# Output stores of a one-core attention and MLP kernel: from GpSimd's queue to SyncE's, with one add and one transfer for each quarter of a batch

## The chip, the cores and the metric

The kernel runs on one core of one Trainium2 chip. The metric is the device time of one execution in microseconds (us). The engines are called as in the profile: PE is TensorE's matmuls, PEld its weight loads, DVE is VectorE, ACT ScalarE, POOL GpSimd, SP SyncE. "Granted clock" is the share of its full clock that TensorE got.

The kernel before was run many times. At first its times were 780.05 us as the median of 3 runs, 780.04 to 781.94. All runs in this document are called fast: none was 1.5% above the fastest of its kernel. Within "fast", however, the kernel before has two levels, near 780.2 and near 781.8, and this will matter.

## The reference, cut to what matters

```python
B, H, S, Ns, D = (8, 8, 512, 32, 64)          # x: [B,H,S,D], state: [B,H,Ns,D], FP32
a     = softmax(scale * x @ state.T);  xread = a @ state        # per batch and head
a2    = softmax(scale * state @ x.T);  sread = a2 @ x
t     = concatenate([xread, sread], axis=2)                      # -> [B*(S+Ns), H*D] = [4352, 512]
h     = t @ w_in                                                 # 512 -> 2048
g     = h * sigmoid(1.702 * h)
out   = g @ w_out                                                # 2048 -> 512, FP32
```

Each batch gives 512 rows of 512 for x and 32 rows for the state. All eight batches' state rows are treated together, under the key "sr".

Of the kernel before, what the change touches and what calls it, by code (L numbers as in the profile page):

```python
# [14 lines left out]
ALU = mybir.AluOpType  # L15
# [5 lines left out]
def kernel(  # L21
# [31 lines left out]
    nc = tc.nc  # L53

    B, H, S, D = x.shape
    Ns = state.shape[2]
# [11 lines left out]
    HF, HN = NF // 2, DM // 2  # L68
# [4 lines left out]
    out_x = out.rearrange("(b t) n -> b t n", b=B)[:, :S].rearrange("b (c q) n -> b c q n", c=SCH)  # L73
    out_s = out.rearrange("(b t) n -> b t n", b=B)[:, S:]
# [43 lines left out]
    def load_state(b):  # L118
        stn[b] = apool.tile([P, NG, D], FP32, tag="stn", name=f"stn_{b}", bufs=2)
        for g in range(NG):  # L120
            nc.sync.dma_start(stn[b][:, g], st_v[b, g])  # L121

    def load_x(b):
        if b == 1:
            xn[b] = sums[:, 0].rearrange("p (c h d) -> p c h d", c=SCH, h=H)
        else:
            xn[b] = xpool.tile([P, SCH, H, D], FP32, tag="xn", name=f"xn_{b}")
        for c in range(SCH):
            nc.sync.dma_start(xn[b][:, c], x_v[b, c])  # L129
# [252 lines left out]
    def att_slots(b):  # L382

        slots = [[] for _ in range(14)]

        def at(i, fn, *args):
            slots[i].append((fn, args))

        at(0, att_state, b)
        for j in range(NPR):  # L390
            at(j, att_xT, b, j)

        at(5, att_scores, b)
        at(5, att_M, b, 0)
        at(5, att_M, b, 1, True)
        at(5, att_blocks, b)
        at(5, att_s_max, b)
        at(5, att_s_exp, b)
        at(5, att_x_exp, b)
        at(5, att_s_norm, b)  # L400
        at(5, att_x_norm, b)
        at(8, att_M, b, 2)
        at(8, att_M, b, 3, True)
        for g in range(NG):
            at(10 + g, att_eT, b, g)
        at(12, att_sread, b)
        at(13, att_srT, b)
        return slots
# [13 lines left out]
    def up_x(b, f, spare=False):  # L422
        c, o = divmod(P * f, FC)
        m = A[b]["M", c]
        up(b, f, S, [m[:, g, o : o + P] for g in range(NG)], [A[b]["aT"][:, g] for g in range(NG)], spare)

    def up_s(f):
        up(
            "sr", f, B * Ns,
            [w_in_of(k, f) for k in range(NPR)],  # L430
            [srT[:, k].rearrange("p b n -> p (b n)") for k in range(NPR)],
        )
# [3 lines left out]
    def down(key, r, fs, dst, last):  # L436

        if fs[0] == 0:
            O[key, r] = psO.tile([P, DM], FP32, tag="o", name=f"o_{key}_{r}")
        ops = O[key, r]  # L440
        for f in fs:
            nc.tensor.matmul(  # L442
                ops, G[key, f][:, P * r : P * (r + 1)], w_out[:, f], start=(f == 0), stop=(f == NF - 1)
            )
            if last and f < HF:
                free.append(G.pop((key, f)))
        if fs[-1] == NF - 1:
            osb = opool.tile([P, DM], FP32, tag="osb", name=f"osb_{key}_{r}")
            nc.scalar.copy(osb, ops)
            nc.gpsimd.dma_start(dst, osb)  # L450


    S1, S2 = (later[:, 4 * i : 4 * i + 4].rearrange("p f n -> p (f n)").rearrange("p (f t) -> p f t", f=HF) for i in range(2))
# [2 lines left out]
    def quarters(key, f, ntok):  # L456

        g, half = G[key, f], ntok // 2
        return g[:, :half], g[:, half:ntok]

    def sums_of_g(key, f, ntok):

        half = ntok // 2
        (a11, a21), (_, a22) = quarters(key, f, ntok), quarters(key, HF + f, ntok)
        s1, s2 = S1[:, f, :half], S2[:, f, :half]
        nc.vector.tensor_tensor(out=s1, in0=a21, in1=a22, op=ALU.add)  # L466
        nc.vector.tensor_tensor(out=a21, in0=a11, in1=a21, op=ALU.subtract)
        nc.vector.tensor_tensor(out=s2, in0=s1, in1=a11, op=ALU.subtract)

    def strassen(key, ntok, dst, slots=None):  # L470
        half = ntok // 2
        nb = half // P
        B11, B21, B22 = w_out[:, :HF, :HN], w_out[:, HF:, :HN], w_out[:, HF:, HN:]
        T3 = w_out[:, :HF, HN:]
        A = lambda i, k: [quarters(key, HF * k + f, ntok)[i] for f in range(HF)]
        S = lambda t: [t[:, f, :half] for f in range(HF)]
        todo = list(slots or [])

        def bank(name):
            return psO.tile([P, nb, HN], FP32, tag="o", name=f"{name}_{key}")  # L480

        def product(ps, lhs, rhs, first):
            for r in range(nb):
                for f in range(HF):
                    nc.tensor.matmul(  # L485
                        ps[:, r], lhs[f][:, P * r : P * (r + 1)], rhs[:, f],
                        start=(first and r == 0 and f == 0), stop=(f == HF - 1), skip_group_check=True,
                    )
                if todo:
                    for fn, args in todo.pop(0):  # L490
                        fn(*args)

        def kept(t):
            return t[:, : nb * HN].rearrange("p (r n) -> p r n", r=nb)

        def store(i, k, ps, with_):

            o = opool.tile([P, nb, HN], FP32, tag="osb", name=f"osb_{key}_{i}{k}")
            for r in range(nb):
                if with_ is None:  # L500
                    nc.scalar.copy(o[:, r], ps[:, r])  # L501
                else:
                    nc.vector.tensor_tensor(out=o[:, r], in0=ps[:, r], in1=with_[:, r], op=ALU.add)  # L503
                nc.gpsimd.dma_start(dst(nb * i + r, slice(HN * k, HN * (k + 1))), o[:, r])  # L504

        k1, k2, k3 = kept(p1), kept(u2), kept(u3)
        X = bank("x")
        product(X, A(0, 0), B11, True)
        nc.scalar.copy(k1, X)
        Y = bank("y")  # L510
        product(Y, S(S2), T2, True)
        nc.vector.tensor_tensor(out=k2, in0=Y, in1=k1, op=ALU.add)  # L512
        product(X, A(0, 1), B21, False)
        store(0, 0, X, None)
        for f in range(HF):
            a12 = quarters(key, HF + f, ntok)[0]
            nc.vector.tensor_tensor(out=a12, in0=a12, in1=S2[:, f, :half], op=ALU.subtract)
        product(Y, A(1, 0), T3, False)
        nc.vector.tensor_tensor(out=k3, in0=Y, in1=k1, op=ALU.add)
        for f in range(HF):  # L520
            free.append(G[key, f])
        Z = bank("z")
        product(Z, S(S1), T1, True)
        store(1, 1, Z, k3)
        product(Y, A(1, 1), T4, False)
        store(1, 0, Y, k1)
        product(Z, A(0, 1), B22, False)
        store(0, 1, Z, k2)
        for f in range(HF, NF):
            free.append(G[key, f])  # L530
# [86 lines left out]
    for f in range(NF):  # L617
        rounds(1)
        round_to(NFC * NPR + f + 1)
        for r in range(SCH):  # L620
            down(0, r, [f], out_x[0, r], r == SCH - 1)
        if f in (0, 2):
            for g in range(NG):
                att_eT(f // 2, g)
        if f in (0, nper * 2):
            att_M(1, 2 + f // (nper * 2))
        if f in (1, 3):
            att_sread(f // 2)
        if f in (2, 4):
            att_srT(f // 2 - 1)  # L630
        if f % 2 == 1:
            up_x(1, rest.pop(0))
        if f == NF - 2:
            T_of(T1, B12, B11)
            for k in range(HF - 1):
                sums_of_g(1, k, S)
            T_of(T2, B22, T1)
# [6 lines left out]
    nb = P // Ns  # L644
    for b in range(1, B):
        ahead = b + 1 < B
        if not ahead:
            for f in range(NF):
                up_s(f)
                if f >= HF:  # L650
                    sums_of_g("sr", f - HF, B * Ns)
            strassen("sr", B * Ns, lambda r, n: out_s[nb * r : nb * (r + 1), :, n])
        if b > 1:
            for f in range(NF):
                up_x(b, f)
                if f >= HF:
                    sums_of_g(b, f - HF, S)
        strassen(b, S, lambda r, n: out_x[b, r][:, n], att_slots(b + 1) if ahead else None)
        if b + 2 < B:
            load_state(b + 2)  # L660
            load_x(b + 2)
# [30 lines left out]
```

## The kernel before: the parts that the change touches

A batch's loads are issued from SyncE's queue. The x of a batch takes four transfers of 256 KB, the state two of 32 KB:

```python
def load_state(b):
    stn[b] = apool.tile([P, NG, D], FP32, tag="stn", name=f"stn_{b}", bufs=2)
    for g in range(NG):
        nc.sync.dma_start(stn[b][:, g], st_v[b, g])
def load_x(b):
    ...                                       # xpool has one buffer; b == 1 lies elsewhere
    for c in range(SCH):
        nc.sync.dma_start(xn[b][:, c], x_v[b, c])
```

Batch 0's second layer is computed directly (`down`); each of its four row blocks is copied out of PSUM by ScalarE and stored by GpSimd. All other batches use Strassen's scheme, which yields the output in quarters (128 partitions, 2 row blocks, 256 columns). Each quarter is stored as two halves:

```python
# in down():
        osb = opool.tile([P, DM], FP32, tag="osb", name=f"osb_{key}_{r}")   # opool: 2 buffers
        nc.scalar.copy(osb, ops)
        nc.gpsimd.dma_start(dst, osb)
# in strassen():
    def store(i, k, ps, with_):
        o = opool.tile([P, nb, HN], FP32, tag="osb", name=f"osb_{key}_{i}{k}")
        for r in range(nb):
            if with_ is None:
                nc.scalar.copy(o[:, r], ps[:, r])
            else:
                nc.vector.tensor_tensor(out=o[:, r], in0=ps[:, r], in1=with_[:, r], op=ALU.add)
            nc.gpsimd.dma_start(dst(nb * i + r, slice(HN * k, HN * (k + 1))), o[:, r])
```

The order in which the program emits the parts around batch 2's first use is this:

```python
for f in range(NF):                            # second layer of batch 0, NF = 16
    rounds(1); round_to(NFC * NPR + f + 1)     # last weights: loaded on SyncE, rounded
    for r in range(SCH):
        down(0, r, [f], out_x[0, r], r == SCH - 1)   # f == 15 stores
    ...
load_state(2)                                  # emitted AFTER batch 0's four stores
load_x(2)
for b in range(1, B):
    ...
    strassen(b, S, ..., att_slots(b + 1))      # the slots hold the next batch's attention:
    if b + 2 < B:                              # slot 0 transposes its state and x on PE
        load_state(b + 2)
        load_x(b + 2)
```

## Time and profile before

| what | kernel before, profiled run |
|---|---|
| device time of the profiled run; span of its trace | 782.2 us; 780.4 us |
| PE busy; mean granted clock | 763.8 us (98%); 0.995 |
| DVE, ACT, POOL busy | 314.4, 219.1, 35.9 us |
| PE's last matmul ends; span ends | 772.50; 780.41 (7.91 us later) |
| stores: POOL | 60 (56 of 128 KB, 4 of 256 KB), and 4 of the state rows |
| loads of batch 2: issued; used | 123 to 128; 165.6 |

The span begins with the first instruction and ends with the last; the device time is 1.7 to 2.1 us longer in all runs here. The stretch from PE's last matmul to the end of the span is called the tail below: 7.91 us here. The profile's lines for the stores, the tail, SP's queue and the stretch near 160 us are shown in the prediction.

One view was not opened before the prediction, and should have been. It is the table of windows: the busy time of each engine, then the granted clock (the third number from the right), the DMA share and GB/s.

```profile
42.00:43.00 1.00, 0.40 (x1) 0.32 (x2) 0.93 (x3) 1.00 (x3) 0.00 (x0) 0.92 0.00 0
44.00:45.00 1.00, 1.00 (x2) 0.33 (x1) 0.96 (x3) 0.00 (x0) 0.00 (x0) 0.50 0.00 0
46.00:47.00 1.00, 1.00 (x4) 0.52 (x3) 1.00 (x4) 0.77 (x2) 0.00 (x0) 0.88 0.00 0
```

The clock is halved from 42.8 to 46.2, 3.4 us (a window at 0.92 has 0.16 us of half clock in it, one at 0.88 has 0.24), after a gap of 2.1 us on PE (40.5 to 42.6). So the profiled run belongs to the upper level, while the median from which the prediction set out, 780.05, belongs to the lower.

### The profile page before, as it was taken

What the parts mean: (1) busy time and instruction counts of PE and PEld (TensorE: products, weight loads), DVE (VectorE), ACT (ScalarE), POOL (GpSimd) and SP (SyncE); (2) the same over time, 40 slices, a digit from 0 to 9 for tenths busy, and PEclk for the clock granted to TensorE, in tenths of its full rate; (3) what the DMA queues carried; (4) which work ended last, traced back from release to release, by engine and by line L of the source; (5) the groups of instructions that cost most, each with busy time, mean ns of one, the idle gap of its engine ahead of it and who ended that gap; (6) DMA issues with size and microseconds to landing.
All of it is one profiled execution on the core that took longest, in us unless ns stands there. A gap on an engine that the chain in (4) does not pass through costs nothing.

```text
span 780.4 us, 9330 instructions
## 1 busy us (share of the span) xinstructions
PE 763.8 (98%) x3883; PEld 509.1 (65%) x3883; DVE 314.4 (40%) x669; ACT 219.1 (28%) x394; POOL 35.9 (5%) x72
## 2 busy tenths in 40 slices
PE   8989999999999999999999999999999999999995
PEld 3433444477855786487847785587748788874885
DVE  5998799534304160317113440407031611313120
ACT  4666511023132132314132313314232312113000
POOL 0000000010100011000100010001100010010011
PEclk9999999999999999999999999999999999999999
DMA  9821245010030003000210013000300000010001
GB/s 229 316 82 51 84 142 136 0 55 12 30 71 1 1 28 85 0 1 14 66 33 0 1 35 78 1 1 28 81 0 1 14 28 14 1 28 1 0 21 34
DMA packets 43626, 35.21 MB, mean 45 GB/s; under 512 B 37312, under 2 KB 37312, under 8 KB 43584
## 3 DMA queue, kind: packets, MB, share of 16 engines
q1 hardware_dynamic: 40000, 25.69, 12.1%
q0 software_dynamic: 3584, 8.92, 3.5%
q8 instruction: 30, 0.49, 0.3%
q14 instruction: 12, 0.10, 0.0%
HBM read 25.69 MB, written 8.91 MB: 44 GB/s over the span
## 4 chain that ended last, share of the span: by engine, by line
issue 69%; PE 22%; POOL 4%; SPq 2%; ACT 1%; DMA 1%; POOLq 0%; DVE 0%; ACTq 0%
PE h L417 8%; PE o L442 7%; POOL out_dram L504 4%; PE y L485 2%; PE x L485 2%; PE M L274 1%; SPq L129 1%; PE z L485 1%; PE warm L113 1%; DMA sums<-in_x_dram 1%; PE xT L256 0%; SPq L121 0%; PE s L274 0%; SPq L158 0%; ACT later L186 0%
## 5 line engine op out<-in xcount | busy, mean ns | idle before, releaser
L417 PE MATMUL h<-aT,M 128*128 128x512 f32 x512 | 225.7, 598 | 4.4 <-ACT M L349 4.4
L417 PEld LDWEIGHTS h<-aT,M 128*128 128x128 f32 x512 | 96.7, 191 | 127.3 <-issue 114.2
L419 ACT ACTIVATE g<-h 128x512 f32<-128x512 f32 x120 | 71.4, 596 | 161.9 <-PE h L417 161.8
L485 PE MATMUL x<-w_out,g 128*128 128x256 f32 x448 | 100.0, 379 | 0.0
L485 PEld LDWEIGHTS x<-w_out,g 128*128 128x128 f32 x448 | 84.2, 190 | 13.9 <-issue 3.3
L466 DVE TENSOR_TENSOR later<-g,g 128x256 f32<-128x256 f32 (+1 forms) x64 | 26.1, 408 | 149.7 <-ACT g L419 149.7
L349 ACT COPY M<-M 128x512 f32<-128x512 f32 x64 | 33.2, 596 | 94.9 <-PE M L274 94.9
L504 POOL DMA_DIRECT2D out_dram<-osb x56 | 30.0, 541 | 528.3 <-ACT osb L501 360.2
L485 PE MATMUL z<-w_out,g 128*128 128x256 f32 x224 | 51.1, 382 | 0.0
L485 PE MATMUL z<-sums,later 128*128 128x256 f32 x224 | 51.1, 382 | 0.0
L485 PE MATMUL y<-sums,later 128*128 128x256 f32 x224 | 50.5, 379 | 0.0
L485 PE MATMUL y<-sums,g 128*128 128x256 f32 x224 | 50.5, 379 | 0.0
L485 PE MATMUL y<-w_out,g 128*128 128x256 f32 x224 | 50.1, 382 | 0.0
L485 PEld LDWEIGHTS y<-w_out,g 128*128 128x128 f32 x224 | 42.1, 190 | 10.5 <-issue 5.0
L485 PEld LDWEIGHTS z<-sums,later 128*128 128x128 f32 x224 | 42.1, 190 | 10.5 <-issue 5.0
L485 PEld LDWEIGHTS y<-sums,g 128*128 128x128 f32 x224 | 42.1, 190 | 5.5
L485 PEld LDWEIGHTS z<-w_out,g 128*128 128x128 f32 x224 | 41.6, 190 | 5.7
L485 PEld LDWEIGHTS y<-sums,later 128*128 128x128 f32 x224 | 41.6, 190 | 5.2
L503 DVE TENSOR_TENSOR osb<-z,later 128x256 f32<-128x256 f32 x28 | 10.6, 419 | 78.6 <-PE z L485 78.6
L512 DVE TENSOR_TENSOR later<-y,later 128x512 f32<-128x512 f32 x7 | 4.8, 691 | 87.8 <-PE y L485 87.8
L274 PE MATMUL M<-w_in,stT 64*32 64x512 f32 x512 | 33.2, 594 | 0.2 <-ACT eT L359 0.2
L257 ACT COPY xT<-xT 128x512 f32<-128x512 f32 x28 | 16.4, 586 | 59.1 <-PE xT L256 59.1
(111 smaller groups left out, 707.1 us busy)
## 6 DMA issues: line engine op xcount, KB each, us to landing
later<-in_moe_w_out_dram SPq DMA_DIRECT2D x16, 512.0 KB
xn<-in_x_dram SPq DMA_DIRECT2D x28, 256.0 KB
out_dram<-osb POOLq DMA_DIRECT2D x56, 128.0 KB, 2.0
w_out<-in_moe_w_in_dram SPq DMA_DIRECT2D x12, 512.0 KB
later<-in_moe_w_in_dram SPq DMA_DIRECT2D x4, 512.0 KB
sums<-in_x_dram SPq DMA_DIRECT2D x4, 256.0 KB
out_dram<-osb POOLq DMA_DIRECT2D x4, 256.0 KB, 2.4
stn<-in_state_dram SPq DMA_DIRECT2D x16, 32.0 KB
```

The lines of the kernel that those rows point to most:

```text
L113: nc.tensor.matmul(ps, zeros[:, :P], zeros, start=True, stop=True)
L129: nc.sync.dma_start(xn[b][:, c], x_v[b, c])
L257: nc.scalar.copy(A[b]["xT"][:, j], ps.rearrange("p c q -> p (c q)"))
L274: nc.tensor.matmul(ps[g][st], A[b]["stT"][rows, st], rhs(rows, j), start=True, stop=True)
L349: nc.scalar.copy(m[:, g], ps[g])
L417: nc.tensor.matmul(hps, lhs[i], rhs[i], start=(i == 0), stop=(i == n - 1))
L419: nc.scalar.activation(out=gt[:, :ntok], in_=hps, func=AF.Gelu_apprx_sigmoid)
L442: nc.tensor.matmul(ops, G[key, f][:, P * r : P * (r + 1)], w_out[:, f], start=(f == 0), stop=(f == NF - 1))
L466: nc.vector.tensor_tensor(out=s1, in0=a21, in1=a22, op=ALU.add)
L485: nc.tensor.matmul(ps[:, r], lhs[f][:, P * r : P * (r + 1)], rhs[:, f], start=(first and r == 0 and f == 0), stop=(f == HF - 1), skip_grou ...
L503: nc.vector.tensor_tensor(out=o[:, r], in0=ps[:, r], in1=with_[:, r], op=ALU.add)
L504: nc.gpsimd.dma_start(dst(nb * i + r, slice(HN * k, HN * (k + 1))), o[:, r])
```

## The change

The intent is to take the stores off GpSimd's queue, which the page lists as `software_dynamic` (8.92 MB before), and to halve the number of adds and transfers. The adding lines and the place of the loads stay as they are.

```diff
@@ down
             nc.scalar.copy(osb, ops)
-            nc.gpsimd.dma_start(dst, osb)
+            nc.sync.dma_start(dst, osb)
@@ strassen, store
-            for r in range(nb):
-                if with_ is None:
-                    nc.scalar.copy(o[:, r], ps[:, r])
-                else:
-                    nc.vector.tensor_tensor(out=o[:, r], in0=ps[:, r], in1=with_[:, r], op=ALU.add)
-                nc.gpsimd.dma_start(dst(nb * i + r, slice(HN * k, HN * (k + 1))), o[:, r])
+            if with_ is None:
+                nc.scalar.copy(o, ps)
+            else:
+                nc.vector.tensor_tensor(out=o, in0=ps, in1=with_, op=ALU.add)
+            nc.sync.dma_start(dst(slice(nb * i, nb * (i + 1)), slice(HN * k, HN * (k + 1))), o)
@@ the two callers: dst takes a slice of row blocks instead of a number
```

More of the change, by code (lines that the diff above doesn't have):

```diff
@@ L651 @@
                     sums_of_g("sr", f - HF, B * Ns)
-            strassen("sr", B * Ns, lambda r, n: out_s[nb * r : nb * (r + 1), :, n])
+            strassen("sr", B * Ns, lambda r, n: out_s[nb * r.start : nb * r.stop, :, n])
         if b > 1:
@@ L657 @@
                     sums_of_g(b, f - HF, S)
-        strassen(b, S, lambda r, n: out_x[b, r][:, n], att_slots(b + 1) if ahead else None)
+        strassen(b, S, lambda r, n: out_x[b, r, :, n].rearrange("r q n -> q r n"), att_slots(b + 1) if ahead else None)
         if b + 2 < B:
```

## The prediction

> **What bounds the kernel now.** I read the page's busy times first, then the clock, then who waits for whom, then the order of time in the three places the change touches.

> ```profile
> PE 763.8 (98%) x3883; PEld 509.1 (65%) x3883; DVE 314.4 (40%) x669; ACT 219.1 (28%) x394; POOL 35.9 (5%) x72
> PE   8989999999999999999999999999999999999995
> ...
> L504 POOL DMA_DIRECT2D out_dram<-osb x56 | 30.0, 541 | 528.3 <-ACT osb L501 360.2
> ```

> TensorE (PE) is busy in every slice from the fourth to the last but one, at a granted clock of 0.995. Busy PE is not proof of a bound, but the list of waits has no wait of PE on a store, on VectorE's (DVE's) adds or on the copies by ScalarE (ACT) into `osb`. GpSimd (POOL), with 60 stores of 0.54 to 0.73 us, is idle 95% of the span. The chain that ended last runs along the POOL stores and calls 69% of the span "issue". That is the walk back from the last instruction staying on POOL between two stores, not a bound: those gaps are POOL waiting for PE's results through DVE and ACT. So the time is PE's stream, plus what follows its last matmul, and a change that touches only stores can act in two ways: shorten the tail, or hold PE up.

> The tail, in order of time and then in the groups of the closing line:

> ```profile
> 769.75 2.75 PE L485 MATMUL z<-w_out,g 128*128 128x256 f32 x12
> ...
> 772.54 0.75 DVE L503 TENSOR_TENSOR osb<-z,later 128x256 f32<-128x256 f32 x2 [6.09 <-PE z L485]
> 773.26 1.07 POOL L504 DMA_DIRECT2D out_dram<-osb  x2 [5.78 <-DVE osb L503]
> ```

> ```profile
> L687 SPq DRAIN  x3: 7/7/13, 776.4 to 779.9; - x3
> L687 POOLq DRAIN  x3: 45/102/5883, 773.7 to 780.1; - x3
> ```

> PE ends at 772.5, the last add at 773.3, the last store's issue at 774.3. In windows of 1 us the DMA moves 148 and 115 GB/s in 774 to 776, nothing after. SyncE (SP), which waits for the stores, begins its first DRAIN at 776.4: everything has landed. Yet the span ends at 780.4. The 5.88 us DRAIN must be POOL's first, since one starting after 774.5 would pass the end; so it lasts from 773.8 to 779.7, and POOL's barrier semaphores start at 779.7. From 776.4 to 779.7 the core waits for POOL alone, and 0.7 us of barrier follows.

> **Where the queue matters.** The loads of the next batches are on SP:

> ```profile
> 50.34 72.61 SPq L158 DMA_DIRECT2D later<-in_moe_w_out_dram  x16
> 123.00 1.13 SPq L121 DMA_DIRECT2D stn<-in_state_dram  x2
> 124.17 3.71 SPq L129 DMA_DIRECT2D xn<-in_x_dram  x4
> 127.93 1.70 SPq L121 DMA_DIRECT2D stn<-in_state_dram  x2
> 216.04 2.91 SPq L129 DMA_DIRECT2D xn<-in_x_dram  x4
> ```

> Batch 2's state and x are issued at 123 and 124, as soon as the weights are through. The stores of batch 0, which stand before them in the program, are made 35 us later but on another queue, so they do not hold them. Now the stretch where batch 0's output leaves and batch 2 is first used:

> ```profile
> 158.04 0.58 ACT L449 COPY osb<-o 128x512 f32<-128x512 f32 x1 [3.69 <-PE o L442]
> 158.94 0.68 POOL L450 DMA_DIRECT2D out_dram<-osb  x1 [157.56 <-ACT osb L449]
> 161.50 0.58 ACT L449 COPY osb<-o 128x512 f32<-128x512 f32 x1 [2.01 <-DMA out_dram<-osb]
> 162.38 0.59 ACT L449 COPY osb<-o 128x512 f32<-128x512 f32 x1 [0.30 <-PE h L417]
> 163.26 0.54 POOL L450 DMA_DIRECT2D out_dram<-osb  x1 [0.34 <-ACT osb L449]
> 165.59 0.27 PE L247 MATMUL stT<-ident,stn 128*128 128x128 f32 x1
> 165.70 0.60 PE L256 MATMUL xT<-ident,xn 128*128 128x128 f32 x4
> ```

> With two `osb` buffers, the third copy waits for the first store's landing (158.94 to 161.50: 2.56 us), so the fourth store is issued only at 163.26. Some 2.4 us later PE transposes batch 2's state and then x, which lay there for over 30 us.

> [...] Hence a store that waits on SP holds all issues behind it. The trace agrees: SP waits up to 83.7 us for PE's `sr` at the x loads, and the stn loads behind come after (216.04, then 219.00). [...] the store issued at 158.94 has no traffic in 159 to 160 and 262 GB/s in 160 to 161; SP's loads issued at 216.04 show 0 in the next window and 174 GB/s in 217 to 218, so 1.1 to 1.2 us for both. I use that. [...] PE ends at 772.5 and the clock falls in 776 to 777.

> **The change part by part.**

> 1. *One add of 512 columns for two of 256.* 21 pairs of adds: a pair takes 0.75 to 0.76, the 128x512 add from PSUM at L512 takes 0.69 (4.8/7), so 0.07 us less each, 1.5 us of DVE in all. The pair's copies on ACT go from 0.65 to 0.59, seven times, 0.4 us. DVE is 40% and ACT 28% busy; PE waits for neither. On the path only the last add counts: 0.07 us gained, but the last half-store may no longer start early. In the trace it hardly does so: POOL starts at 773.26, when the second add is nearly done (773.29).

> 2. *28 transfers for 56, 256 KB instead of 128.* SP's issue is 0.5 to 0.9 us each, beside other work. Not on the path but at the end.

> 3. *The tail.* PE end 772.54 + add 0.69 = 773.23; SP's issue with some 0.1 to 0.3 to start, 773.4; landing after 2.4 to 2.56 (256 KB rows on the page: 2.4; line 450: 2.56), 775.9; POOL has long been drained; barrier 0.7 (779.7 to 780.4): 776.7. **Gain 3.7 us**, nearly all of it POOL's DRAIN.

> 4. *The order on SP.* The built kernel's SP queue has, after the last weight load: four stores of batch 0, stn of 2, x of 2. So these loads move from 123 to behind the fourth store. That store keeps its time, 163.26, as ACT's copies keep theirs (perhaps 0.3 earlier). Then its issue, 0.55: 163.8. Two stn loads at the 1.13 of the row at 123.00: 164.9. Four x loads start at 164.9; first data after 1.1: 166.0; 1.05 MB at 235 GB/s (mean of the windows 126 to 130, where these same loads ran) is 4.5: 170.5; completion and wake-up, estimated from the store's traffic end near 161.3 against 161.50, 0.2 to 0.3: 170.7. The first x transposes need all four chunks; the fourth ran at about 166.2. **PE stalls 4.5 us**, in pieces as state and chunks arrive. PE is the bound everywhere after, so all of it is lost.

> 5. *Later batches.* There, x loads waited for `sr` (216.04); now they also stand behind the last store, whose add ends at 220.4, and the stn loads: some 6 us later, landing near 229. PE needs them after the up products end at 246.3. Hidden, with 17 us to spare, in all five of the later loads.

> 6. *The clock.* [...] three or four transposes fall inside it[...]: I give one in seven to a half clock costing some 2 us, 0.3 on average.

> Sum: 780.05 - 3.7 + 4.5 + 0.3 = 781.15; I say 781.2.

> **Rivals.**

> - *The tail alone counts* (batch 2's loads come in time): 776.4, 0.5% faster. It would need them issued by about 160. The built order speaks against it, as the third store cannot pass before the first has landed.
> - *The stall is much longer*: stores hold SP longer than GpSimd, or stn and x go slower beside the last store; with the clock halved[...]. Stall 7 and clock 3: 786. The load rate of this trace speaks against it.
> - *The tail gains nothing*, because the wait at the end belongs to the program's end and not to POOL's stores: 784.9. Against it: SP, DVE and ACT drains take under 1 us, and POOL's has 5.88 right after its last store.
> - *Every later batch stalls too.* Five stalls of even 3 us would give 796, 2% slower. Against it stand 17 us of slack (point 5).

> **Range and chances.** Stall 3 to 6, tail 2.5 to 4.3, clock 0 to 2 give 778.7 at best and 785.5 at worst if all go one way; eight in ten: 778.3 to 784.8, with the runs' own spread (780.04 to 781.94) in mind. 2% is 15.6 us, which only repeated stalls would reach: slower 2%; faster by that needs more than the whole tail: under 1%; within 2%, 97%.

> **What would show it.** In the profile after: SP's stn and x loads of batch 2 at 164 to 168 instead of 123; PE's transposes of `stT` and `xT` waiting for those DMAs near 166 to 171, the first waits of PE on a DMA since the start; everything after shifted by that stall; the later x loads at some 4 to 6 us behind, with no wait of PE; POOL without rows after the start; the span ending within 1 us of SP's wait for the last store, some 4 us after PE's last matmul instead of 7.9; DVE busy 1.5 us less. It is wrong if PE has no gap near 166 (time near 776), or POOL's DRAIN remains (785), or PE waits in later batches.

## The result, and the profile after

The changed kernel took **785.49 us** (median of 4 runs, 784.18 to 786.15), the kernel before 780.08 (median of 4 runs, 780.04 to 781.94). The ratio is 1.0061, 95% interval 1.0042 to 1.0081: within 2%, but clearly slower, and 0.7 us above the predicted range. A ratio in this document is the mean time of one kernel's fast runs over that of the other's of the same rounds, so it is not quite the ratio of the medians.

Three rows of the page after: busy times, granted clock in 40 slices, and the chain that ended last.

```profile
PE 766.8 (98%) x3881; PEld 510.9 (65%) x3883; DVE 312.7 (40%) x648; ACT 218.8 (28%) x387; POOL 0.8 (0%) x8
...
PEclk9999999989999999999999999999999999999999
...
PE 94%; SPq 2%; DMA 1%; ACT 1%; issue 0%; DVE 0%; ACTq 0%
```

POOL has only its eight set-up instructions left. The chain now shows PE itself, as it no longer ends in POOL's stores. There is a dent in the clock in slice 9, the stretch from 157 to 176 us.

SP's queue after, in order of time (start, duration, what):

```profile
158.17 3.94 SPq L450 DMA_DIRECT2D out_dram<-osb  x4
162.21 1.13 SPq L121 DMA_DIRECT2D stn<-in_state_dram  x2
163.44 3.00 SPq L129 DMA_DIRECT2D xn<-in_x_dram  x4
...
228.83 2.82 SPq L129 DMA_DIRECT2D xn<-in_x_dram  x4
```

Batch 2's loads are issued 39 us later than before, straight behind batch 0's four stores. Batch 3's x moved from 216 to 229. What PE makes of it (start, duration, what; in brackets the idle time before and what ended it):

```profile
165.46 0.30 PE L247 MATMUL stT<-ident,stn 128*128 128x128 f32 x1 [0.19 <-DMA stn<-in_state_dram]
166.97 0.30 PE L256 MATMUL xT<-ident,xn 128*128 128x128 f32 x1 [1.21 <-DMA xn<-in_x_dram]
...
169.28 0.48 PE L256 MATMUL xT<-ident,xn 128*128 128x128 f32 x1 [0.87 <-DMA xn<-in_x_dram]
170.41 0.47 PE L256 MATMUL xT<-ident,xn 128*128 128x128 f32 x1 [0.65 <-DMA xn<-in_x_dram]
170.68 5.84 PE L485 MATMUL x<-w_out,g 128*128 128x256 f32 x16
```

PE meets the chunks of x one at a time as they land. `x` here is also the name of Strassen's first product of batch 1: its first half (16 records of PE) runs, then come batch 2's transposes of `stT` and `xT`, then its second half. In the kernel before, the two halves of this product began 4.00 us apart (162.13 and 166.13). Here they begin at 161.65 and 170.68, which is 9.03: **5.0 us of stall**. Then the second half's 16 records take 5.84 us instead of 3.62: **2.2 us more**, for the same work. The windows of the same stretch say why:

```profile
167.00:168.00 1.00, 0.27 (x1) 0.08 (x1) 1.00 (x1) 0.00 (x0) 0.00 (x0) 1.00 1.28 221
168.00:169.00 1.00, 0.33 (x1) 0.14 (x1) 0.10 (x1) 0.00 (x0) 0.00 (x0) 0.67 1.34 222
171.00:172.00 1.00, 1.00 (x4) 0.73 (x4) 0.00 (x0) 0.51 (x1) 0.00 (x0) 0.50 0.00 0
175.00:176.00 1.00, 1.00 (x6) 0.90 (x5) 0.00 (x0) 0.00 (x0) 0.00 (x0) 0.91 0.06 16
```

The clock falls to half at 168.3, in the middle of the stall, though PE has a transpose in nearly every microsecond. It stays there until 175.2, 4.5 us after PE is full again: 6.8 us in all. Half of these 4.5 us is 2.25, the size of the loss.

The tail, first in order of time and then in the group of the closing line:

```profile
772.20 7.07 PE L485 MATMUL z<-w_out,g 128*128 128x256 f32 x32
...
779.31 0.69 DVE L502 TENSOR_TENSOR osb<-z,later 128x512 f32<-128x512 f32 x1 [6.16 <-PE z L485]
```

```profile
L686 POOLq DRAIN  x3: 34/78/459, 1.0 to 783.1; - x3
L686 SPq DRAIN  x3: 7/7/13, 782.6 to 782.9; - x3
```

PE ends at 779.27, SP has its last store by 782.6, and the span ends at 783.3. POOL's DRAINs are now under 0.5 us. (A DRAIN here is an instruction near the end of an engine's program: PE's ends at 779.3 and VectorE's at 780.1, when their own last work is done.) The tail is 4.06 us instead of 7.91. The sum for the two traces: 5.03 + 2.22 of PE, less 3.85 of tail, less 0.48 by which this run happened to be ahead at 162: +2.9, the difference of the spans (780.41 to 783.33).

The medians are 5.4 us apart, however, not 2.9. Both profiled runs contain the early half clock near 43. Of the kernel before, the median run doesn't; of the changed one, three runs of four have the mean clock of the profiled run (0.993), and the fourth, at 784.18, has 0.995. The experiments test this reading too.

### The profile page after: what moved, and what is told of

The parts are those of the page before. It is cut to its first block, busy times and chain, and to the rows that moved or that the text cites. A ratio compares the mean times of both kernels' runs of the same rounds, so it can differ in the third digit from the quotient of the medians.

```text
span 783.3 us, 9205 instructions
## 1 busy us (share of the span) xinstructions
PE 766.8 (98%) x3881; PEld 510.9 (65%) x3883; DVE 312.7 (40%) x648; ACT 218.8 (28%) x387; POOL 0.8 (0%) x8
## 4 chain that ended last, share of the span: by engine, by line
PE 94%; SPq 2%; DMA 1%; ACT 1%; issue 0%; DVE 0%; ACTq 0%
PE h L417 28%; PE y L485 19%; PE z L485 13%; PE x L485 12%; PE o L442 7%; PE M L274 4%; PE h_sr L417 4%; PE xT L256 2%; SPq L129 1%; PE y_sr L485 1%; PE sr L369 1%; PE s L274 1%; PE z_sr L485 1%; PE x_sr L485 1%; PE warm L113 1%; PE eT L358 1%
## 5 line engine op out<-in xcount | busy, mean ns | idle before, releaser
L417 PE MATMUL h<-aT,M 128*128 128x512 f32 x512 | 225.6, 597 | 4.4 <-ACT M L349 4.4
L417 PEld LDWEIGHTS h<-aT,M 128*128 128x128 f32 x512 | 96.8, 191 | 127.1 <-issue 114.0
L485 PE MATMUL x<-w_out,g 128*128 128x256 f32 x448 | 102.2, 385 | 0.0
L485 PEld LDWEIGHTS x<-w_out,g 128*128 128x128 f32 x448 | 85.9, 194 | 14.6 <-issue 3.3
L485 PE MATMUL z<-w_out,g 128*128 128x256 f32 x224 | 51.1, 382 | 0.0
L485 PE MATMUL z<-sums,later 128*128 128x256 f32 x224 | 51.1, 382 | 0.0
L485 PE MATMUL y<-sums,later 128*128 128x256 f32 x224 | 50.5, 379 | 0.0
L485 PE MATMUL y<-sums,g 128*128 128x256 f32 x224 | 50.5, 379 | 0.0
L485 PE MATMUL y<-w_out,g 128*128 128x256 f32 x224 | 50.1, 382 | 0.0
L485 PEld LDWEIGHTS z<-sums,later 128*128 128x128 f32 x224 | 42.1, 190 | 10.5 <-issue 5.0
L485 PEld LDWEIGHTS y<-w_out,g 128*128 128x128 f32 x224 | 42.1, 190 | 10.5 <-issue 5.0
L485 PEld LDWEIGHTS y<-sums,g 128*128 128x128 f32 x224 | 42.1, 190 | 5.5
L485 PEld LDWEIGHTS z<-w_out,g 128*128 128x128 f32 x224 | 41.6, 190 | 5.7
L485 PEld LDWEIGHTS y<-sums,later 128*128 128x128 f32 x224 | 41.6, 190 | 5.2
L502 DVE TENSOR_TENSOR osb<-z,later 128x512 f32<-128x512 f32 x14 | 9.7, 692 | 79.6 <-PE z L485 79.6
L287 DVE STREAM_TRANSPOSE e<-s 128x512 f32<-128x512 f32 x16 | 10.5, 695 | 46.1 <-PE s L274 46.1
```

The lines of the kernel that those rows point to most:

```text
L287: nc.vector.transpose(t[:, g].rearrange("p i n -> p (i n)"), a["s"][g])
L417: nc.tensor.matmul(hps, lhs[i], rhs[i], start=(i == 0), stop=(i == n - 1))
L485: nc.tensor.matmul(ps[:, r], lhs[f][:, P * r : P * (r + 1)], rhs[:, f], start=(first and r == 0 and f == 0), stop=(f == HF - 1), skip_grou ...
L502: nc.vector.tensor_tensor(out=o, in0=ps, in1=with_, op=ALU.add)
```

## The experiments

Theory: the four stores of batch 0 hold batch 2's loads on SP; this stalls PE by 5 us, and the stall halves its clock, which costs some 2 us more; the end of POOL's DRAIN gives 3.8 us back; and a half clock near 43, which comes and goes by chance, makes both kernels' times spread. Rivals: the merged adds and transfers carry part of it; the lost clock has nothing to do with the stall; the tail's gain has another cause. Eleven kernels ran, each correct. The first eight share one chip; the last three ran on another. Each was timed in 5 rounds beside the kernel before.

| run | median us | range | kernel before, median | ratio (95%) |
|---|---|---|---|---|
| loads_first | 776.83 | 776.16 to 776.96 | 780.41 | 0.9945 (0.9932 to 0.9958) |
| queue_only | 784.78 | 783.31 to 785.29 | 780.41 | 1.0044 (1.0031 to 1.0056) |
| merge_only | 779.78 | 779.38 to 780.65 | 780.41 | 0.9985 (0.9973 to 0.9997) |
| warm_in_stall | 785.16 | 784.82 to 787.18 | 780.41 | 1.0060 (1.0047 to 1.0073) |
| early_warm | 780.02 | 779.81 to 780.06 | 781.0 | 0.9987 (0.9972 to 1.0001) |
| after_early_warm | 783.68 | 783.41 to 784.09 | 781.0 | 1.0035 (1.0021 to 1.0050) |
| warm_in_stall_5 | 781.35 | 781.09 to 781.77 | 781.0 | 1.0005 (0.9992 to 1.0018) |
| last_store_only | 776.11 | 775.97 to 776.55 | 781.0 | 0.9938 (0.9925 to 0.9951) |
| batch0_on_gpsimd | 776.39 | 776.08 to 777.43 | 780.38 | 0.9943 (0.9930 to 0.9957) |
| best | 776.55 | 776.33 to 777.52 | 780.38 | 0.9945 (0.9932 to 0.9958) |
| best_split | 776.26 | 775.77 to 777.10 | 780.38 | 0.9939 (0.9925 to 0.9953) |

### loads_first

```diff
 # on the changed kernel
     for f in range(NF):
         ...
+        if f == NF - 1:
+            load_state(2)
+            load_x(2)
         for r in range(SCH):
             down(0, r, [f], out_x[0, r], r == SCH - 1)
     ...
-    load_state(2)
-    load_x(2)
```

> The changed kernel with one edit: batch 2's state and x loads are emitted before the four stores of batch 0 instead of after them. Theory (the stores on SyncE's queue hold these loads, PE stalls 4.6 us near 166 and its clock halves for 6.8 us, while the tail is 3.9 us shorter): loads issued at 123 again, no wait of PE near 166, no half clock there, tail of some 4.0 us from PE's last matmul to the end; time some 4 us under the kernel before, near 776. Rival (the merged adds or hardware stores slow PE in some other way, and the loads' place is incidental): time stays near 783 to 785.

Measured: 776.83 us, 8.7 us under the changed kernel's first median (6.9 under after_early_warm below, its clean counterpart on the same chip) and 3.6 under the kernel before. SP's queue and PE in order of time:

```profile
122.51 4.01 SPq L129 DMA_DIRECT2D xn<-in_x_dram  x4
156.98 3.96 SPq L450 DMA_DIRECT2D out_dram<-osb  x4
```

```profile
164.02 0.60 PE L256 MATMUL xT<-ident,xn 128*128 128x128 f32 x4
164.46 3.62 PE L485 MATMUL x<-w_out,g 128*128 128x256 f32 x16
```

The loads go out 34 us before the stores, PE has no bracket of waiting, and the second half of `x` takes its 3.62 us. The windows show a half clock only at the end. The stall and the half clock near 168 hang on the loads' place in the queue; the rival falls.

### queue_only

```diff
 # on the kernel before, in down() and in store()
-            nc.gpsimd.dma_start(dst, osb)
+            nc.sync.dma_start(dst, osb)
-                nc.gpsimd.dma_start(dst(nb * i + r, ...), o[:, r])
+                nc.sync.dma_start(dst(nb * i + r, ...), o[:, r])
```

> The kernel before with the stores moved to SyncE and nothing else: two adds and two transfers per quarter as before. Theory (the queue does it all): the same stall near 166, the same half clock, the same short tail, 784 to 786. Rival (the single add and the 256 KB transfer carry part of the cost): nearer to 780 to 782.

Measured: 784.78 us. In its trace, SP's x loads of batch 2 start at 163.45, the halves of `x` at 161.66 and 170.63 (5.0 us of stall), and the second half takes 6.37 us at half clock. So the queue does it, and the merge isn't needed for the loss. The tail is 3.52 us here and 4.06 in the changed kernel. With two adds and two transfers SP issues the first half 0.45 us after VectorE starts on the adds (779.78 to 780.23), with one of each 0.72 us after (779.31 to 780.03). On SP's queue the merge thus makes the end some 0.5 us longer (0.26 of it comes from the order in which SP looks at its semaphores: four more after the last store's, against none).

### merge_only

```diff
 # on the changed kernel, both places
-            nc.sync.dma_start(dst..., o)
+            nc.gpsimd.dma_start(dst..., o)
```

> The changed kernel with its stores back on GpSimd: one add and one transfer per quarter, but the old queue. Theory (the merge is off the path, the GpSimd DRAIN at the end stays): within 0.5 us of the kernel before, 780, tail near 7.9 us. Rival (the merge costs at the end, or gains by halving the issues on GpSimd): a tail different by over 1 us.

Measured: 779.78 us, formally inside what the theory expected. But the profile shows that its reason was wrong, and the rival's mark, a tail different by over 1 us, is there. The closing line's group:

```profile
L686 POOLq DRAIN  x3: 40/102/4187, 772.9 to 777.5; - x3
```

POOL's DRAIN is 4.19 us instead of 5.88. PE's last matmul ends at 771.85 and the span at 777.84: a tail of 5.99, not 7.91. So the merge alone takes 1.9 us off the tail, when the queue stays on GpSimd. The time hardly shows it, because this kernel's profiled run has the early half clock (42.5 to 46.0). With it, 780.02 (early_warm below) - 1.9 + 1.5 = 779.6 is what the five runs should be near, and they lie at 779.38 to 780.65; without it they would be near 778.1. That all five were of the upper level is likely from this, not shown.

### warm_in_stall

```diff
 # on the changed kernel, in att_slots
+        def hold(n):
+            ps = psH.tile([P, FC], FP32, tag="h", name="hold")
+            for _ in range(n):
+                nc.tensor.matmul(ps, w_in[0][:, 0, :P], w_in[0][:, 0], start=True, stop=True)
+        if b == 2:
+            at(0, hold, 10)
         at(0, att_state, b)
```

> The changed kernel with ten matmuls of no use (0.43 us each) put before batch 2's state transpose, so that PE works while it would wait for the loads. Theory (stall 4.6 us and, on top, a half clock[...] that costs 2.4 us): the stall's length stays, as the loads come no sooner, but the clock stays full from 166 to 176; some 2.4 us faster than the changed kernel, near 783. Rival (the clock falls whatever PE does, or the lost time is the stall alone): no faster than 785.

Measured: 785.16 us, a miss by 2 us. The mean clock was 0.999 in the profiled run and stayed full from 163 to 176, as the theory expected, but no time was won, which is where the rival put it. The line of PE:

```profile
163.69 8.75 PE L392 MATMUL hold<-w_in 128*128 128x512 f32 x20
```

The ten matmuls are twenty records of 0.43 us. These FP32 matmuls take two records each, as the kernel's own FP32 products do (half of `x`: 8 matmuls, 16 records); its transposes take one (four of `xT` at 164.02 in loads_first: x4), the bf16 fillers too (`keep_warm(11)` at 1.19 in the kernel before: x11). I had overlooked this. The filler ran 8.75 us, in place of a stall of 5 and a clock loss of 2.2. Here work in the gap kept the clock up (1.00 from 163 to 176, where the trace after has 0.5 from 168.3 to 175.2); for the time it was inconclusive and was repeated with half the filler, below.

### early_warm

```diff
 # on the kernel before
     att_M(1, 0)
+    keep_warm(8)          # bf16 matmuls of 0.22 us into a PSUM bank that nobody reads
     def turn(...)
```

> The kernel before with eight filler matmuls (0.22 us each) in PE's 2.1 us gap near 40.5, which ends in a half clock from 42.3 to 45.8 in the profiled run. Theory (the two levels of the kernel before, 780.3 and 781.8, are runs without and with this half clock, and which one comes is the chance of where the gap falls): all runs at the lower level, 780.0 to 780.5, clock 0.998, none at 781.8. Rival (the levels have another cause): still both levels.

Measured: 780.02 us, and all four runs between 779.81 and 780.06. The kernel before, in its twelve runs on this chip, had six at 780.08 to 780.41 and six at 781.58 to 781.87. The windows of the run with the filler:

```profile
40.00:44.00 4.00, 3.56 (x15) 1.56 (x14) 3.93 (x9) 2.54 (x5) 0.00 (x0) 1.00 0.01 2
44.00:48.00 4.00, 4.00 (x11) 1.85 (x10) 3.86 (x8) 3.78 (x7) 0.00 (x0) 1.00 0.02 4
```

The clock is full where the kernel before has 0.5 in its profiled run, and the upper level is gone. The two levels are executions without and with this half clock, 1.5 us apart (means 780.26 and 781.72). That it comes by chance is shown by loads_first: its profiled run has the same PE gap of 2.12 us (40.5 to 42.6) and no half clock there. Of the kernel before's 27 runs 12 were at the upper level.

The traces also show when the clock changed. It is read from their windows of 1 us, in which a granted clock between 0.5 and 1 tells how much of the window was at half. Five traces have a half clock before the last one:

| run | clock falls to 0.5, us | lasts, us | full stretch up to the next fall, us |
|---|---|---|---|
| before | 42.83 | 3.41 | 730.45 |
| merge_only | 42.54 | 3.4 | 730.4 |
| after | 42.05 | 3.41 | 122.9 |
| after | 168.35 | 6.83 | 607.57 |
| queue_only | 43.06 | 3.4 | 122.9 |
| queue_only | 169.36 | 6.8 | 607.6 |
| after_early_warm | 169.40 | 3.4 | 607.6 |

| run | step, us | PE busy share | clock in the step | clock in the next |
|---|---|---|---|---|
| before | 39.42 to 42.83 | 0.38 | full | half |
| loads_first | 37.77 to 41.18 | 0.80 | full | full |
| loads_first | 41.18 to 44.59 | 0.58 | full | full |
| after | 38.64 to 42.05 | 0.43 | full | half |
| after | 164.93 to 168.35 | 0.35 | full | half |
| after | 168.35 to 171.76 | 0.55 | half | half |
| after | 171.76 to 175.18 | 1.00 | half | full |
| after_early_warm | 165.98 to 169.40 | 0.25 | full | half |
| after_early_warm | 169.40 to 172.81 | 0.99 | half | full |
| queue_only | 165.94 to 169.36 | 0.26 | full | half |
| queue_only | 169.36 to 172.77 | 0.73 | half | half |

In the kernel before, the gap lies within one step (0.38 busy); in loads_first, by that count, it is spread over two, with shares of 0.80 and 0.58. With the steps of the other traces counted in the same way, from 10 us on, the full steps that a half one followed had shares of 0 to 0.43, and those that a full one followed had 0.56 and more; of the half ones, those with 0.55 and 0.73 were followed by a half one, those with 0.95 to 1.00 by a full one. This is what these 13 traces hold and no more: between these shares nothing was measured, and the share counts a PE that works as busy, whatever part of its array a matmul uses (the products `M` before the gap use 64 by 32). It was worked out from the traces after the runs, and no experiment was made to test it.

### after_early_warm

```diff
 # on the changed kernel
     att_M(1, 0)
+    keep_warm(8)
     def turn(...)
```

> The changed kernel with the same eight filler matmuls near 40.5. Theory (785.5 is 784 plus the early half clock in three of four runs; 784 is stall 4.6 plus half clock 2.4 to 2.6 minus tail 3.7 over 780.3): all runs at 783.5 to 784.3. Rival (the early half clock has nothing to do with it): 785.5 as before.

Measured: 783.68 us, four runs from 783.41 to 784.09. That leaves a clean pair: 783.68 against 780.02, **3.7 us slower**. In the traces, the halves of `x` begin 8.95 us apart (160.73 and 169.68) instead of 4.00, and PE's line reads

```profile
169.68 5.17 PE L485 MATMUL x<-w_out,g 128*128 128x256 f32 x16
```

so the stall is 4.95 and the half clock (169.4 to 172.8 here) costs 1.55. Tail: 4.06 against 7.91, a gain of 3.85. Sum: 4.95 + 1.55 - 3.85 = 2.65. The spans differ by 3.4, as this run's PE was 0.76 behind at 160 already, before any of it; such a start-up spread goes both ways (the changed kernel's first trace was 0.48 ahead).

### warm_in_stall_5

```diff
 # on after_early_warm, in att_slots: hold as above
+        if b == 2:
+            at(0, hold, 5)
         at(0, att_state, b)
```

> As after_early_warm, with five useless matmuls (an FP32 one runs as two records of 0.43 us, so 4.3 us; the run with ten put in 8.75 us, almost twice the stall) before batch 2's state transpose. Theory (stall 4.6 us, and the half clock on top of it worth 2.4 us): clock full throughout, 2.2 to 2.6 us under after_early_warm, near 781.5. Rival (the stall alone): equal to after_early_warm.

Measured: 781.35 us, 2.3 us under after_early_warm, and clocks of 0.999 to 1.0. PE's lines:

```profile
163.23 4.46 PE L392 MATMUL hold<-w_in 128*128 128x512 f32 x10
...
168.44 0.33 PE L256 MATMUL xT<-ident,xn 128*128 128x128 f32 x1 [0.32 <-DMA xn<-in_x_dram]
168.60 3.62 PE L492 MATMUL x<-w_out,g 128*128 128x256 f32 x16
```

Useless work in the gap leaves the stall (the halves are 8.82 apart, 4.8 more than undisturbed) but not the half clock, and the second half takes its 3.62 us. So of the clean loss on PE some 5 us are waiting and about 2 are clock, and the second part is caused by the idleness of the first. Under the kernel's own clean time of 780.02 this version is 1.3 us slower: 4.82 less the tail's 3.85 is 0.97.

### last_store_only

```diff
 # on the kernel before (with keep_warm(8) as in early_warm)
-                nc.gpsimd.dma_start(dst(nb * i + r, ...), o[:, r])
+                (nc.sync if (key, i, k) == (B - 1, 0, 1) else nc.gpsimd).dma_start(dst(nb * i + r, ...), o[:, r])
```

> The kernel before (with the early filler) in which only the last quarter's two transfers of the last batch go out from SyncE, all others from GpSimd. Theory (GpSimd's DRAIN works off its last stores, 5.9 us after their issue, so it is over if they were issued 6.9 us earlier): DRAIN from 767.5 ends near 773.4, tail 4.0 to 4.4 instead of 7.9 us, time near 776.8. Rival (the DRAIN's length is fixed and it begins at the program's end, or any use of GpSimd's queue costs it): tail stays at 7 to 8 us, 780.

Measured: 776.11 us, 3.9 us under early_warm. The closing line's group, and SP's:

```profile
L688 SPq DRAIN  x3: 7/7/13, 773.3 to 773.7; - x3
L688 POOLq DRAIN  x3: 40/102/5724, 764.6 to 773.9; - x3
```

POOL still has a DRAIN of 5.72 us, but its last two stores were issued from 764.1 to 765.1 and the DRAIN begins amid them, at 764.6 (the theory had 767.5). So it is over by 770.3 and SP's wait for the last store ends the program. The tail from PE's end (770.17) to 774.2 is 4.0. The whole gain of the change at the tail is in the last two of 60 transfers; the other stores can stay where they were.

### batch0_on_gpsimd

```diff
 # on after_early_warm, in down()
-            nc.sync.dma_start(dst, osb)
+            nc.gpsimd.dma_start(dst, osb)
```

> The changed kernel (with the early filler) in which only the four stores of batch 0 go back to GpSimd; the 28 merged stores and the four of the state rows stay on SyncE. Theory (those four stores alone held batch 2's loads, and in later batches the loads behind the stores are hidden): loads at 123, no wait of PE near 166, no half clock but at the end, GpSimd's DRAIN long over, near 776.3. Rival (a part of the stall comes from the 28 later stores): above 778.

Measured: 776.39 us. The x loads of batch 2 start at 121.9, the halves of `x` begin 4.00 us apart (159.85 and 163.85), the clock is below 0.99 only from 774 on. So the four stores of batch 0 alone made the loss, and the 28 later ones on SP cost PE nothing. POOL's longest DRAIN is 2.58 us here and in no one's way.

### best

```diff
 # on loads_first
     att_M(1, 0)
+    keep_warm(8)
     def turn(...)
```

> The changed kernel with batch 2's loads emitted before batch 0's stores and with the early filler: the two causes of loss mended together. Theory: the runs of loads_first were already without the early half clock (clock 1.0), so no faster than they, 776.2 to 777.0, and no run above.

Measured: 776.55 us; one of the six runs, at 777.52, lies above the expected 777.0, and its trace (the profiled run) has no half clock but the last one. What the filler does for the kernel before it needn't do here: loads_first had no run with the early half clock, by luck or otherwise.

### best_split

```diff
 # on best, in store()
+            if (key, i, k) == (B - 1, 0, 1):
+                for r in range(nb):
+                    nc.vector.tensor_tensor(out=o[:, r], in0=ps[:, r], in1=with_[:, r], op=ALU.add)
+                    (nc.sync, nc.scalar)[r].dma_start(dst(slice(r, r + 1), slice(HN * k, HN * (k + 1))), o[:, r : r + 1])
+                return
```

> As best, but the last quarter alone is again two adds and two transfers, the first from SyncE and the second from ScalarE's queue. The tail from PE's end: the first half leaves 0.3 us earlier, the second at the same time but with half the bytes. Theory: 0.3 to 0.6 us under best, near 776.2. Rival (issue and landing are fixed costs, size plays no part): equal to best.

Measured: 776.26 us, 0.3 under best, with ranges that overlap (775.77 to 777.10 against 776.33 to 777.52). By the times, inconclusive; the traces have tails of 3.61 and 4.07 us, 0.46 less with the split, as the theory expected. All five versions without the stall (medians 776.1 to 776.8) can't be told apart by these runs. Each beats the kernel before by an interval that excludes 1, though by less than 2%, and the slowest of all their runs (777.52) is below the changed kernel's fastest (784.18; 783.41 with the early filler).

## Why the prediction was wrong, point by point

**Right: what bounds, the tail, the order on SP, the later batches.** PE waits for x as said, for the first time since the start. The tail is 4.06 us where step 3 has 4.16 (772.54 to 776.7), and the gain 3.85 where it says 3.7. DVE is 1.7 us less busy for the foretold 1.5. Batch 3's x, issued at 228.8, has its traffic over by 235, and PE takes it at 257: 22 us of slack, and no PE wait. But step 1, which had the merge gain 0.07 us at the end, was wrong twice. The merge alone shortens POOL's DRAIN (merge_only: tail 5.99), which counts for nothing in the changed kernel, as its long DRAIN is gone. And on SP's queue the merge costs some 0.5 us at the end (tails of 4.06 against 3.52 in queue_only), because the first half can no longer leave early.

**Step 4, the stall: mechanism right, 4.5 foretold, 4.8 to 5.0 measured, from terms that missed in opposite directions.** The prediction took SP's and GpSimd's stores to land equally fast. They don't: on SP, ACT's third copy starts 2.15 us after the first store's issue (158.17 to 160.32), on GpSimd 2.56. The first packet moves 0.84 us after the issue on SP (159.01) and 1.25 on GpSimd (158.94 to 160.19), a difference that step 4's windows of 1 us hid. So the x loads start 1.8 us after `x` begins (161.65 to 163.44), where step 4 has 2.8 (162.13 to 164.9). On the other side, the loads took longer. In the trace after, their last packet ends at 169.65, 6.2 us after the first x load's issue, where step 4 has 5.6 (164.9 to 170.5). And "completion and wake-up" was put at 0.2 to 0.3, but PE runs the fourth chunk at 170.41, 0.76 us after that packet; in warm_in_stall_5 the same, from 167.69 to 168.44. The estimate came from a misread window: near 161.3 two stores' traffic overlaps, and the first store's last packet ended at 161.04, 0.46 before ACT's copy at 161.50.

**Step 6, the clock: this is the step that failed.** It gave "one in seven to a half clock costing some 2 us, 0.3 on average", and counted on three or four transposes inside the stall. That chance was an estimate of mine, which no trace had shown. The transposes, that of the state included, did not hold the clock: it fell in every one of the three traces with the stall (after, queue_only, after_early_warm) and in none of those where PE worked through it or had no stall. In the 3.41 us before the fall PE was busy for 0.25 to 0.35 of the time. The cost was 1.55 to 2.75 us (second half of `x` 5.17, 5.84 and 6.37 instead of 3.62), half of the time that PE then worked at half clock (3.13, 4.50 and 5.55 us). The early gap's steps (see the table of busy shares under early_warm), with PE busy for 0.38 to 0.43 and no transpose among it, were followed by the half clock as well.

**The base of the sum.** The prediction computed from a trace of the upper level (782.2 us, with the half clock near 43) and set out from a median of the lower (780.05). It looked at windows of other stretches and, here, only at the page's tenths, in which slice 3, from 39 to 58.5 us, shows a 9 like all others. The clean pair needs no such correction: 780.02 + 4.95 + 1.55 - 3.85 = 782.7 against 783.68, of which 0.76 is start-up spread in that trace. The first median of the changed kernel, 785.49, is about 1.5 to 2 us above its clean time, the size of the early half clock, which its profiled run has, and two other runs by their clock of 0.993. With the early one left out, the time would have been inside the range; the point was still 2.5 us too low: 1.25 by the clock, 0.45 by the stall, 0.76 by the start-up spread of that trace, which is chance; the tail took 0.15 back, and some 0.2 is the runs' spread.

**Rivals.** "The tail alone counts", 776.4, is what happens when the loads are let through: loads_first, 776.83. "The stall is much longer" named the clock, at 3 us, and gave 786; its stall of 7 was wrong. Its time came close by luck, as the early half clock made up for what the stall lacked.

**Left open.** What sets the length of POOL's DRAIN: 5.88 us after two stores of 128 KB, 4.19 after one of 256 KB, 2.58 after batch 0's stores of 256 KB with rows twice as long. Why all of merge_only's runs seem to have the early half clock, and none of loads_first's: the profiled runs have 0.39 busy in the step before the fall (merge_only) and, by the count above, 0.80 and 0.58 (loads_first), but why five runs in a row should be alike is not shown. Why the changes of the clock lie at other times from run to run, and what follows a share between 0.43 and 0.56. (That the stall's half clock lasted 3.4 us in one trace and 6.8 in the two others goes with the table of busy shares under early_warm: in its first 3.41 us PE was busy for 0.99, and for 0.55 and 0.73.)

## What to carry to other kernels

When a store moves to a queue that also issues loads, list that queue's new order and ask of each load behind a store when the store's data will be ready; emit loads that are free to go before it. Here a PE gap cost its length and then the clock: price a stall of 4 to 5 us with some 2 us more (1.55 to 2.75 in three traces) even if transposes trickle through it, or fill it with matmuls (warm_in_stall_5: 2.3 us less). And before adding up, check that the trace and the time that you start from are of the same kind, by looking at the clock in windows of a microsecond.
